# One more chunk of the MLP's second product as seven half-block products, and another order of all steps

## The chip, the cores and the metric

The kernel runs on one core of a Trainium2 chip. The metric is the device time of one execution in microseconds (us). The core has five queues of instructions: TensorE (PE, matrix products; its weight loads are shown apart as PEld), VectorE (DVE), ScalarE (ACT), GpSimd (POOL) and SyncE (SP), which issues nearly all transfers. Each queue works strictly in the order in which its instructions were written, and semaphores hold an instruction until what it reads is there and what it overwrites has been read.

## The reference

A recurrent attention (4 batches, 8 heads, 768 time steps, head size 40) is followed by a two-layer MLP with an exact GELU (320 to 2048 to 320) over 3072 tokens. The MLP's two weight matrices are of 64-bit floats; everything else is of 32 bits.

```python
for t in range(S):
    y[:, :, t] = np.einsum('bhd,bhde->bhe', rt, state)
    Sa = np.einsum('bhde,bhe->bhd', state, at)
    state_decay = state * wt[:, :, None, :] - np.einsum('bhd,bhe->bhde', Sa, bt)
    state = state_decay + np.einsum('bhd,bhe->bhde', vt, kt)
...
x = np.ascontiguousarray(attn_out.transpose(0, 2, 1, 3)).reshape(B * S, H * D)
...
h = x @ w_in
g = 0.5 * h * (1.0 + erf(h * inv_sqrt2))
return (g @ w_out).astype(np.float32)
```

## The kernel before

The sequence of 768 steps is cut into 12 chunks of 64. In each chunk the recurrence is turned into matrix products, for all 4 batches and 8 heads at once, and the chunk's 256 tokens (4 batches times 64 steps) then go through the MLP.

**Who sets the order.** The function `order` returns one long string of tokens such as `nm.3`, which means step `nm` of chunk 3. `perform` calls the steps in that order, and each writes its instructions to the queue it belongs to. The schedule is manual on all five queues, so the order of the tokens is the order on each queue. The argument `first_seven` (the constant `NS`) isn't used in `order`; what is done how is in the tokens themselves. PSUM is four banks, which `take` and `drop` hand out in the order of the tokens, so the order also decides which step waits for which bank.

**The steps of a chunk**, by their tokens:

- Loads on SP: `Lw La Lb Lk LV Lr` (w, a, b, k, v, r), from chunk 4 on others besides (`Lv Lwt Lbt Lkt`).
- Decays: `lg` (logarithm of w, ACT), `cu` and `wT` (running sums, PE), `ec` and `ew` (exponentials, ACT), `sa sb sk` (products with a, b, k; DVE or POOL). In the early chunks `ta tb tk tv tr` turn tiles over on PE, and `sn kc vc rc` copy them out of PSUM on ACT.
- Small products on PE, each followed by a masked copy on DVE: `nm`/`nk` (the matrix N that has to be inverted), `vm`/`vk`, `am`/`ak`.
- The inverse. For chunk 0 a loop of four squarings and a last product: `qm.0` to `qm.4` on PE, with `qc qz qb qa` on ACT and DVE between them, and `ql` (a transpose, L996) at the end. From chunk 1 on 32x32 blocks go through DRAM (`Ns`, `Nl`) to POOL, which solves them (`ic`, L907 and L909), and back (`Is`, `If`, `Ij`); `tc_` (L1007) turns them, and `jm jc km kt0 kt1` join blocks to 64x64.
- The chunk's result: `av xm` (PE), `xc0 xc1` (copies), `sm` (product with the inverse), `sc` (copies), `pk pb` (new state and output), `oa od om` (DVE), `tm tn oc` (the state turned over for the next chunk), `ym yc`. `om` writes the output, times a decay, into `xt`, the MLP's input, and `ox` completes `xt` with 11 small transfers.
- The MLP: `mh.c.p` for p from 0 to 7 is the first product (L1231, 20 records each in the trace, since each product of 32-bit floats appears as two), `ge` the GELU on ACT. The second product of the first three chunks is `pm.c.0` to `pm.c.3` (L1347: eight matmuls of 128x320 each), copied out by `pc`. From the fourth chunk on it is `m1` to `m7` (L1270): the 2x2 blocks of GELU output and weights go through Winograd's form of Strassen's scheme, seven products of half blocks (eight matmuls of 128x160 each) instead of eight. Its sums are `s1` to `s4` on DVE, `e1` to `e6` on ACT and DVE, and once, for the weights, `ws.0` to `ws.3`. `so` writes the output.

**The weights** come as 64-bit floats. There are 26 units (0 to 9 are the first matrix, 10 to 25 the second), loaded by `Lf`, `Lf5` and `Ls`, and converted with integer operations: `cp cm cs` on DVE and `ce` on ACT, and then in one of three ways: `cv` (two DVE instructions), or `cl cn` (ACT) with `cg` (two POOL instructions), or `cl cn` with `cx` (two products with the identity on PE) and `cy` (one on DVE). Before the change no unit goes the third way, though the steps are there.

**Products of constants.** `warm.4.i` is one matmul of the identity with four copies of a mask (128x512, two records), whose result nobody reads; `warm_first` is three such products.

The lines named here and below: L1231 `mh`, L1236 `ge`, L1270 `m1` to `m7`, L1347 `pm`, L1223 the sums of the seven products, L1220 `ws`, L845 the masked copies, L588 `cp`, L602 `cm`, L609 `cs`, L617 and L618 `cv`, L595 `ce`, L640 and L641 `cg`, L1007 `tc_`, L996 `ql`, L1164 `om`, L1176 and L1179 `ox`. L196 is the helper `mm`, which writes most small products.

```python
def perform(steps, token):
    name, *numbers = token.split(".")
    steps[name](*(int(n) if n.isdigit() else n for n in numbers))
...
    @step
    def warm(n, i):
        pt = take(f"warm{i}")
        mm(pt[:, 0, :n * P], ident, cum_m.unsqueeze(1).to_broadcast([P, n, P]))
        drop(f"warm{i}")
```

Of the kernel before, what the change touches and what calls it, by code (L numbers as in the profile page):

```python
# [16 lines left out]
def order(chunks, first_seven):  # L17
    return """
        of_half_set Lw.0 pads_a.0 sums_mask lg.0 cu.0 ec.0 Lb.0 sb.0 warm_set pads_w.0 pads_extra.2 pads_extra.0
        pads_extra.1 identity upper_mask pads_rows.0 pads_r.0 pads_VR.1 pads_r.1 first_ones.0 Tt_zero bias_set  # L20
        pads_a.1 pads_w.1 first_ones.1 pads_VR.0 wT.0 warm.4.18 ew.0 tb.0 sn.0 La.0 Lf.0.1.0 ta.0 sa.0 nm.0 nk.0
        qt Lw.1 Lf.3.1.0 lg.1 wT.1 ew.1 warm.4.26 qm.0 warm.4.16 cu.1 Lf.1.0.0 Lf.0.0.1 Lf.0.0.0 Lf.3.0.0 cl.3
        Lf.1.1.0 Lf5.1.0 Lb.1 La.1 Lf.2.1.0 Lf.0.1.1 Lf5.0.1 Lk.0 qi.0.p pads_extra.3 qi.1.v cp.1 cp.0 qc.0 ce.1
        qz.0 cm.1 qb.0.0.v qb.0.1.a qm.1 qc.1 cs.1 cv.1 cm.0 cm.3 cp.3 warm_first Lr.0 Lf.2.0.0 Lf5.0.0 LV.0
        Lf.2.0.1 Lf.2.1.1 Lf5.1.1 Lk.1 warm.4.11 qa.1 qz.1 qb.1.0.v ce.0 cn.3 ce.3 ec.1 qb.1.1.a cs.0 cs.3 sb.1
        qm.2 qa.2 qz.2 qb.2.0.v warm.4.3 ta.1 warm.4.19 tb.1 iz.1 cg.3 sk.0.p sa.1 cp.5 cv.0 cm.5 cl.5 qc.2
        qb.2.1.a qm.3 qz.3 qb.3.0.v qa.3 tk.0 ce.5 sn.1 nm.1 kc.0 qb.3.1.a cn.5 nk.1 cs.5 cp.2 tr.0 cg.5 qm.4
        rc.0 ce.2 cl.4 qc.3 cl.7 tv.0 qa.4 cs.2 cp.7 cm.2 ce.7 cm.7 cn.7 ql cs.7 am.0 jm.0 ak.0 cv.2 cp.4 cm.4
# [12 lines left out]
        ce.23 kc.2 cs.23 cv.23 cp.25 pm.0.0 mh.0.6 mh.0.7 cl.20 cn.20 ce.20 cs.20 cm.25 ce.25 cs.25 cv.25 tc_.1
        unused.a unused.v cg.20 ge.0.2 jm.1 vm.2 iz.2 ic.2.0.4 ic.2.4.8 ic.2.8.12 ic.2.12.16 ic.2.16.20
        pads_rows.1 ic.2.20.24 onward_set ic.2.24.28 ic.2.28.31 cp.22 ce.22 cs.22 cm.22 Ls.14 Lw.3 cv.22 cm.24
        jc.1 km.1 vk.2 ge.0.3 kt1.1 La.3 Lr.3 pm.0.1 kt0.1 sm.1 cp.24 unused.r sc.1.1 sc.1.0 lg.3 cu.3 ec.3 ce.24
        ta.3 cs.24 cv.24 am.2 pk.1 pb.1 Lk.3 Lv.3 Lb.3 pm.0.3 pm.0.2 La.4 oa.1.1 om.1.1 oa.1.0 om.1.0 od.1.0 sb.3
        od.1.1 sk.3.v pc.0.1 pc.0.0 ak.2 ox.1.0 ox.1.1 tb.3 tm.1 wT.3 oc.1 sn.3 tn.1 av.2 ym.2 ew.3 yc.2 mh.1.2
        sa.3 tv.3 nm.3 nk.3 xm.2 ta.4 mh.1.3 LV.3 so.0.0 Lwt.4 Ns.3.0 Is.2.0.s Is.2.1.s Ns.3.1 Lb.4 If.2.1 If.2.0
        Ij.2.1 Ij.2.0 so.0.1 Nl.3.1 Nl.3.0 tc_.2 tr.3 Lbt.4 Lr.4 ge.1.1 mh.1.6 mh.1.7 mh.1.0 xc1.2 xc0.2 ge.1.3
        mh.1.4 mh.1.1 ge.1.0 jm.2 tk.3 jc.2 km.2 kt1.2 kt0.2 kc.3 mh.1.5 ge.1.2 sm.2 sc.2.0 sc.2.1 tb.4 pk.2 am.3
        pb.2 tr.4 oa.2.1 pm.1.0 vm.3 oa.2.0 od.2.0 od.2.1 om.2.1 om.2.0 tw.4 ak.3 vk.3 Lb.5 Lw.4 Lkt.4 La.5  # L50
        ox.2.1 Lv.4 LV.4 tm.2 pm.1.1 oc.2 tn.2 lt.4 pw.4 ew.4 en.4 av.3 ym.3 yc.3 sn.4 sa.4 pm.1.3 xm.3 nm.4
        pc.1.1 pm.1.2 ox.2.0 tv.4 xc1.3 nk.4 vm.4 ta.5 pc.1.0 vk.4 tk.4 Ns.4.1 Ns.4.0 so.1.1 mh.2.6 mh.2.0 mh.2.7
        mh.2.2 mh.2.1 xc0.3 lg.4 ge.2.3 iz.3 ic.3.0.4 ic.3.4.8 ic.3.8.12 ic.3.12.16 ic.3.16.20 ic.3.20.24
        ic.3.24.28 ic.3.28.31 Is.3.1.p Is.3.0.p Nl.4.0 Nl.4.1 iz.4 ic.4.0.4 ic.4.4.8 ic.4.8.12 ic.4.12.16
        ic.4.16.20 ic.4.20.24 ic.4.24.28 ic.4.28.31 Is.4.1.p Is.4.0.p iz.5 If.3.1 If.3.0 Lwt.5 Ij.3.1 Ij.3.0 kc.4
        tc_.3 am.4 jm.3 mh.2.3 ge.2.0 jc.3 km.3 tw.5 ak.4 kt1.3 ge.2.1 kt0.3 lt.5 Lr.5 Lk.4 mh.2.4 sm.3 tr.5
        sc.3.1 sc.3.0 mh.2.5 pk.3 pb.3 cu.4 ge.2.2 pw.5 pm.2.0 pm.2.2 oa.3.1 om.3.1 od.3.1 oa.3.0 od.3.0 tm.3
        Lv.5 Lbt.5 Lkt.5 so.1.0 Lw.5 om.3.0 tb.5 oc.3 ec.4 ew.5 en.5 tn.3 av.4 ym.4 yc.4 ws.0 lg.5 sa.5 pc.2.0
        tv.5 sn.5 pm.2.1 nm.5 La.6 ox.3.1 Lk.5 ox.3.0 xm.4 pm.2.3 sk.4.p nk.5 Ns.5.0 Ns.5.1 If.4.0 If.4.1 Nl.5.1
        Nl.5.0 Lwt.6 Ij.4.0 Ij.4.1 xc0.4 tk.5 ws.1 kc.5 xc1.4 one_set vm.5 am.5 vk.5 tc_.4 pc.2.1 ak.5 ta.6  # L60
        mh.3.0 mh.3.1 jm.4 mh.3.6 jc.4 ge.3.0 km.4 kt0.4 mh.3.7 ge.3.3 Lbt.6 Lr.6 kt1.4 sm.4 sc.4.1 sc.4.0 sb.4
        cu.5 mh.3.2 pk.4 pb.4 LV.5 so.2.1 so.2.0 tr.6 tw.6 tb.6 ec.5 lt.6 Lkt.6 mh.3.3 mh.3.4 mh.3.5 ge.3.1
        ge.3.2 m1.3 m2.3 oa.4.0 oa.4.1 od.4.1 ws.3 od.4.0 tm.4 oc.4 tn.4 av.5 ym.5 om.4.0 pw.6 om.4.1 s1.3 s2.3
        s4.3 e1.3 ew.6 Lv.6 La.7 Lw.6 ox.4.1 ic.5.0.4 ic.5.4.8 ic.5.8.12 ic.5.12.16 ic.5.16.20 ic.5.20.24
# [1321 lines left out]
```

## Time and profile before

| what | value |
|---|---|
| median of 3 runs | 672.73 us (672.18 to 674.0) |
| the profiled execution | 673.18 us |
| its span on the core, first to last instruction | 671.5 us |
| mean granted clock of TensorE | 0.982 |
| PE busy | 643.9 us, 96% |
| DVE / ACT / POOL busy | 421.5 / 262.9 / 382.7 us |
| transfers | 78.10 MB, mean 116 GB/s |
| chain that ended last | PE 80%, of it L1231 28%, L196 22%, L1270 21%, L1347 8% |

The costliest groups of PE:

| line | what | records | busy, us |
|---|---|---|---|
| L1231 | first product of the MLP | 1920 | 222.9 |
| L1270 | seven products of nine chunks (four groups) | 1008 | 147.2 |
| L1347 | second product of three chunks | 192 | 54.3 |
| L196 | products of constants (128x512) | 18 | 12.3 |

How to read it: the span is what the profile covers, and the time of an execution is a little longer (673.18 against 671.5 us). A busy time is the union of an engine's instructions; since matmuls overlap, the mean duration of one times their number is more than the busy time. The page also has a picture of the span in 40 equal slices, in which a digit is the busy share in tenths; one slice is 16.8 us. In the answers of the trace "idle before <- X" is the time in which an engine stood before an instruction, and X what ended that time; "issue" means that the profile shows nothing it waited for.

### The profile page before, as it was taken

The page shows a single profiled execution, that of the slowest core. Times are in us where ns is not written, and L with a number is a line of the kernel's source. Part 1 is how long each engine was busy: PE and PEld are TensorE (multiplying, and loading weights), DVE is VectorE, ACT ScalarE, POOL GpSimd, SP SyncE. Part 2 cuts the span into 40 slices and gives each one's busy share as a digit, 9 for nine tenths or more (in the row PEclk, how much of TensorE's full clock was granted, in tenths as well). Part 3 has the DMA queues.
Part 4 walks back from the last instruction along what each step waited for, and adds up shares of the span by engine and source line. Part 5 has one row for each costly group of instructions (what it writes and reads, how often), then busy time and mean ns, then how long its engine had stood idle before and what let it go on. Part 6 is the DMA issues. An engine that isn't in the chain of part 4 may idle for free.

```text
span 671.5 us, 28177 instructions
## 1 busy us (share of the span) xinstructions
PE 643.9 (96%) x12480; PEld 560.8 (84%) x12480; DVE 421.5 (63%) x528; ACT 262.9 (39%) x329; POOL 382.7 (57%) x803
## 2 busy tenths in 40 slices
PE   4797889999999999999999999999999999999997
PEld 3576778888778878898898998997998988988987
DVE  1699988671664755885884777773885863723403
ACT  4456636522352452552623545242252344033040
POOL 4245873780585873871886860884872877830000
PEclk9796979999999999999999999999999999999999
DMA  9989488848867758647949757748658564130100
GB/s 153 159 169 163 98 189 170 152 91 137 151 112 138 137 109 148 138 86 136 155 85 163 141 115 136 124 86 155 130 108 141 109 121 84 38 60 3 26 16 21
DMA packets 302934, 78.10 MB, mean 116 GB/s; under 512 B 282556, under 2 KB 297692, under 8 KB 302812
## 3 DMA queue, kind: packets, MB, share of 16 engines
q1 hardware_dynamic: 301748, 73.78, 60.2%
q0 software_dynamic: 864, 2.36, 2.1%
q8 instruction: 98, 1.61, 1.0%
q14 instruction: 24, 0.20, 0.1%
q10 hardware_dynamic: 200, 0.16, 0.1%
HBM read 62.62 MB, written 9.70 MB: 108 GB/s over the span
## 4 chain that ended last, share of the span: by engine, by line
PE 80%; DVE 4%; SPq 2%; DMA 2%; issue 2%; POOL 1%; ACT 1%; DVEq 0%; POOLq 0%; ACTq 0%
PE bank L1231 28%; PE bank L196 22%; PE bank L1270 21%; PE bank L1347 8%; PE bank L731 2%; DMA v_pairs<-in_w_dram 1%; SPq L446 1%; POOL tmp L907 1%; DVE conv L609 1%; DMA T<-inv_blocks 1%; POOL W L909 1%; SPq L886 1%; DVE conv L588 0%; DVE kT L737 0%; DVE conv L602 0%
## 5 line engine op out<-in xcount | busy, mean ns | idle before, releaser
L1231 PE MATMUL bank<-xt,w_in_sb 64*128 64x256 f32 x1920 | 222.9, 384 | 0.1
L1231 PEld LDWEIGHTS bank<-xt,w_in_sb 64*128 64x128 f32 x1920 | 182.9, 188 | 25.2 <-issue 2.1
L907 POOL TENSOR_TENSOR tmp<-W,Nb 128x126 f32<-128x126 f32 (+22 forms) x341 | 151.7, 445 | 91.0 <-DMA Nb<-N_blocks 65.2
L909 POOL TENSOR_TENSOR W<-W,tmp 128x126 f32<-128x126 f32 (+22 forms) x341 | 160.4, 470 | 26.7
L1236 ACT ACTIVATE gt<-bank 128x1024 f32<-128x1024 f32 x48 | 48.9, 1023 | 104.5 <-PE bank L1231 104.4
L1270 PE MATMUL bank<-w_out_sb,gt 128*128 128x160 f32 x576 | 83.7, 301 | 0.0
L1270 PEld LDWEIGHTS bank<-w_out_sb,gt 128*128 128x128 f32 x576 | 79.2, 190 | 3.0 <-issue 2.0
L1347 PE MATMUL bank<-w_out_sb,gt 128*128 128x320 f32 x192 | 54.3, 437 | 0.7 <-issue 0.7
L1347 PEld LDWEIGHTS bank<-w_out_sb,gt 128*128 128x128 f32 x192 | 35.7, 190 | 15.6 <-issue 1.4
L1108 DVE TENSOR_TENSOR SM<-bank,upper 128x832 f32<-128x832 f32 x24 | 23.7, 1019 | 19.4 <-PE bank L196 19.3
L1007 DVE STREAM_TRANSPOSE conv<-Tt 128x512 f32<-128x512 f32 x11 | 7.8, 709 | 36.5 <-DMA Tt<-inv_blocks 36.4
L1056 DVE COPY Tt<-bank 32x512 f32<-32x512 f32 x9 | 6.2, 689 | 34.4 <-ACT Tt L1056 32.9
L898 POOL MEMSET W<- 128x512 f32 x11 | 5.8, 530 | 38.2 <-DMA inv_blocks<-W 38.2
L701 DVE TENSOR_TENSOR_SCAN kT<-spare,kT 128x256 f32<-128x256 f32 x32 | 24.1, 813 | 3.5 <-ACT kT L694 3.5
L1270 PE MATMUL bank<-extra,conv 128*128 128x160 f32 x176 | 25.7, 300 | 0.0
L1223 DVE TENSOR_TENSOR os<-os,bank 128x160 f32<-128x160 f32 x36 | 11.4, 318 | 22.6 <-PE bank L1270 12.1
L1158 DVE TENSOR_TENSOR st<-bank,st 128x832 f32<-128x832 f32 (+1 forms) x22 | 21.0, 981 | 6.4 <-PE bank L196 6.4
L1270 PEld LDWEIGHTS bank<-extra,conv 128*128 128x128 f32 x176 | 24.4, 190 | 0.2
L1223 DVE TENSOR_TENSOR conv<-gt 128x1024 f32<-128x1024 f32 x9 | 11.7, 1297 | 20.3 <-ACT gt L1236 20.3
L595 ACT ACTIVATE conv<-conv,rebias 128x320 uint32<-128x320 uint32 (+1 forms) x26 | 16.0, 622 | 21.2 <-DVE conv L588 21.2
L196 PEld LDWEIGHTS bank<-SM,Tt 64*64 64x64 f32 x768 | 17.5, 133 | 6.2 <-issue 3.4
L1236 ACT ACT_TABLE_LOAD x17 | 21.8, 1283 | 1.1 <-DVE N L845 0.8
(212 smaller groups left out, 1120.4 us busy)
## 6 DMA issues: line engine op xcount, KB each, us to landing
Nb<-N_blocks SPq DMA_DIRECT2D x22, 256.0 KB
b_rows<-in_b_dram SPq DMA_DIRECT2D x24, 160.0 KB
k_rows<-in_k_dram SPq DMA_DIRECT2D x24, 160.0 KB
VR<-in_v_dram SPq DMA_DIRECT2D x24, 160.0 KB
out_dram<-os SPq DMA_DIRECT2D x48, 80.0 KB
Tt<-inv_blocks SPq DMA_DIRECT2D x44, 64.0 KB
a_pairs<-in_a_dram SPq DMA_DIRECT2D x18, 144.0 KB
r_pairs<-in_r_dram SPq DMA_DIRECT2D x36, 72.0 KB
```

The lines of the kernel that those rows point to most:

```text
L196: nc.tensor.matmul(o, lhsT, rhs, start=first, stop=True, skip_group_check=True)
L595: nc.scalar.activation(power, power, ACT.Relu, bias=rebias, scale=8.0)
L701: nc.vector.tensor_tensor_scan(logs[:, at:at + n], onward, logs[:, at:at + n], 0.0, ALU.mult, ALU.add)
L907: nc.gpsimd.tensor_tensor(t, W[:, :rows, j:j + 1].to_broadcast([P, rows, rest]), Nb[:, j:j + 1, j + 1:].to_broadcast([P, rows, rest]), ALU ...
L909: nc.gpsimd.tensor_tensor(W[:, :rows, j + 1:], W[:, :rows, j + 1:], t, ALU.add)
L1108: nc.vector.tensor_tensor(SM[:, g], pair_of(f"S{c}_", g).rearrange("p x i c -> p i x c"), pass_upper.unsqueeze(1).unsqueeze(1).to_broadcas ...
L1158: nc.vector.tensor_tensor(to, pair_of(f"QY{c}_", g)[:, :, :, cols], to, ALU.add)
L1223: nc.vector.tensor_tensor(to, one_, other, how)
L1231: nc.tensor.matmul(ph[:, x, s], w_in_sb[half(x), kt, p * P:(p + 1) * P], xt[half(x), kt], start=kt == 0, stop=kt == NK - 1)
L1236: nc.scalar.activation(gt[:, 4 * q:4 * q + 4].rearrange("p (x s) t -> p x s t", x=2), bank(f"ph{c}_{q}").rearrange("p x (s t) -> p x s t", ...
L1270: nc.tensor.matmul(po[:, n, :DM // 2], l_[:, f], r_[:, f], start=f == 0, stop=f == NF // 2 - 1)
L1347: nc.tensor.matmul(po[:, g, :DM], gt[:, f, g * P:(g + 1) * P], w_out_sb[:, f], start=f == 0, stop=f == NF - 1)
```

## The change

Nothing is changed but the string of tokens and the constant `NS`. The string holds 1515 tokens before and 1535 after. As sets they differ in this:

```
removed   pm.2.0 pm.2.1 pm.2.2 pm.2.3  pc.2.0 pc.2.1
added     m1.2 to m7.2  s1.2 to s4.2  e1.2 to e6.2
removed   warm: three of 9        added   warm: twelve, 18 in all
units 0, 11      cv            becomes  cl cn cx cy
unit 8           cv            becomes  cl cn cg
units 5, 9, 16, 21   cl cn cg  become   cv
```

All the other tokens are the same, in another order. The diff, cut to its core:

```diff
-        of_half_set Lw.0 pads_a.0 sums_mask lg.0 cu.0 ec.0 Lb.0 sb.0 warm_set pads_w.0 pads_extra.2 pads_extra.0
...
+        identity sums_mask warm.4.7 Lf.0.1.0 Lf.0.0.0 cm.0 cp.0 warm.4.5 cn.0 cl.0 warm.4.9 warm.4.1 warm.4.28
+        of_half_set pads_VR.1 warm.4.27 warm_set pads_VR.0 onward_set cx.0 warm_first Lw.0 first_ones.0 bias_set
...
-    NS = 3
+    NS = 2
```

The order on PE, up to the first products of the second chunk's join, as it follows from the two strings:

```
before  cu.0 wT.0 warm.18 tb.0 ta.0 nm.0 wT.1 warm.26 qm.0 warm.16 cu.1 qm.1 warm_first warm.11 qm.2 warm.3 ta.1
        warm.19 tb.1 qm.3 tk.0 nm.1 tr.0 qm.4 tv.0 am.0 jm.0 warm.10 vm.0 km.0 av.0 sm.0 pk.0 pb.0
        wT.2 tk.1 tm.0 warm.29 cu.2 tr.1 tv.1 ta.2 warm.12 am.1 vm.1 mh.0.2 mh.0.3 av.1 ym.1 mh.0.0 tb.2 xm.1
        nm.2 mh.0.1 tv.2 mh.0.4 mh.0.5 tr.2 tk.2 pm.0.0 mh.0.6 mh.0.7 jm.1
after   warm.7 warm.5 warm.9 warm.1 warm.28 warm.27 cx.0 warm_first cu.0 wT.0 ta.0 tb.0 nm.0 warm.20 warm.26 tk.0
        qm.0 warm.11 warm.0 warm.25 qm.1 cu.1 wT.1 am.0 qm.2 warm.3 tv.0 qm.3 warm.21 ta.1 tb.1 qm.4 tr.0 nm.1
        vm.0 jm.0 tr.1 av.0 km.0 warm.29 tv.1 sm.0 tk.1 vm.1 warm.10 pk.0 pb.0
        am.1 cu.2 wT.2 warm.16 cx.11 tm.0 av.1 ym.1 warm.23 tb.2 ta.2 tr.2 xm.1 nm.2 mh.0.2 mh.0.3 mh.0.0 mh.0.6
        mh.0.7 mh.0.1 mh.0.4 mh.0.5 tv.2 pm.0.0 pm.0.1 jm.1
```

On DVE, from the inverse loop to the first chunk's output `om.0`:

```
before  qz.0 cm.1 qb.0 cs.1 cv.1 cm.0 cm.3 cp.3 qa.1 qz.1 qb.1 cs.0 cs.3 sb.1 qa.2 qz.2 qb.2 sa.1 cp.5 cv.0 cm.5
        qz.3 qb.3 qa.3 nk.1 cs.5 cp.2 qa.4 cs.2 cp.7 cm.2 cm.7 ql cs.7 ak.0 cv.2 cp.4 cm.4 cp.9 vk.0 cs.4 cm.9
        kt1.0 sk.1 cs.9 xc1.0 cm.6 cp.6 cs.6 sc.0.1 sc.0.0 cv.6 od.0 od.0 om.0.1 cp.8 om.0.0
after   qz.0 cm.1 qb.0 cs.1 cv.1 qz.1 cs.2 qa.1 cm.2 qb.1 cm.3 cp.3 cv.2 cs.3 qa.2 qz.2 qb.2 sb.1 cp.4 cm.4 cp.5
        qa.3 qz.3 cm.5 cs.4 qb.3 sa.1 cs.5 cv.5 qa.4 ql cp.6 nk.1 cm.7 vk.0 ak.0 cm.6 cs.6 cp.7 cv.6 cs.7 cm.8
        cp.8 xc1.0 kt1.0 sk.1 cm.9 cs.8 cp.9 sc.0.1 sc.0.0 cs.9 cv.9 vk.1 cp.11 cp.10 od.0 om.0.0 om.0.1
```

On SP, up to the transfers that complete the first chunk's `xt`:

```
before  Lw.0 Lb.0 La.0 Lf.0.1.0 Lw.1 Lf.3.1.0 Lf.1.0.0 Lf.0.0.1 Lf.0.0.0 Lf.3.0.0 Lf.1.1.0 Lf5.1.0 Lb.1 La.1
        Lf.2.1.0 Lf.0.1.1 Lf5.0.1 Lk.0 Lr.0 Lf.2.0.0 Lf5.0.0 LV.0 Lf.2.0.1 Lf.2.1.1 Lf5.1.1 Lk.1 Ls.2 Ns.1.1
        Lf.1.0.1 Lf.1.1.1 Ns.1.0 Lw.2 Lf.3.1.1 Nl.1.0 Nl.1.1 Ls.0 Lf.3.0.1 Lr.1 LV.1 Ls.1 Ls.3 La.2 ox.0.1 ox.0.0
after   Lf.0.1.0 Lf.0.0.0 Lw.0 La.0 Lb.0 Lk.0 Lf.1.1.0 Lf.2.1.0 Lf.2.0.0 Lf.1.0.0 Lw.1 Lf5.0.0 Lf.3.1.0 Lf.0.1.1
        Lf.3.0.0 LV.0 Lf5.0.1 Lf.0.0.1 Lf.3.0.1 Lb.1 La.1 Lf.1.1.1 Lf5.1.0 Lr.0 Lf.2.0.1 Lf.2.1.1 Lf.1.0.1 Lf.3.1.1
        Lr.1 LV.1 Lf5.1.1 Lk.1 Ns.1.1 Ns.1.0 Ls.0 Ls.1 Lw.2 Nl.1.0 Nl.1.1 Lr.2 Ls.3 Ls.4 Ls.2 Lb.2 La.2 ox.0.1 Ls.5
        ox.0.0
```

On PE around chunk 2's second product:

```
before  pk.3 pb.3 cu.4 pm.2.0 pm.2.2 tm.3 av.4 ym.4 pm.2.1 nm.5 xm.4 pm.2.3 vm.5 am.5 mh.3.0
after   pk.3 pb.3 mh.2.4 mh.2.5 m1.2 m2.2 tm.3 m5.2 av.4 ym.4 m6.2 xm.4 nm.5 mh.3.0 mh.3.1 m3.2 m7.2 m4.2 vm.5 am.5
```

## The prediction

> **What bounds the kernel now.** I read first the page's sums and slices, then stretches of 4 us over the start, then TensorE's (PE's) instructions in order of time, then the chain of waits.
>
> ```profile
> span 671.5 us, 28177 instructions
> ...
> PE 643.9 (96%) x12480; PEld 560.8 (84%) x12480; DVE 421.5 (63%) x528; ACT 262.9 (39%) x329; POOL 382.7 (57%) x803
> ...
> PE   4797889999999999999999999999999999999997
> ...
> DVE  1699988671664755885884777773885863723403
> ...
> DMA  9989488848867758647949757748658564130100
> GB/s 153 159 169 163 98 189 170 152 91 137 151 112 138 137 109 148 138 86 136 155 85 163 141 115 136 124 86 155 130 108 141 109 121 84 38 60 3 26 16 21
> ```
>
> A slice is 16.8 us. PE idles 27.6 us (671.5 - 643.9). In the stretches of 10 us 20.6 of them lie before 100 us, 4.2 behind the last product, and only 2.8 between. So from 105 us on the time is the sum of PE's work, and all else is the start. There the DMA engines are nearly full for 67 us (mean 161 GB/s) and VectorE (DVE) is 84 to 99% busy from 40 to 100 us.
>
> ```profile
> 20.00:24.00 4.00, 0.32 (x6) 0.14 (x5) 3.92 (x5) 0.78 (x2) 3.77 (x6) 0.92 1.12 124
> 24.00:28.00 4.00, 3.62 (x125) 2.62 (x126) 1.08 (x4) 1.50 (x3) 0.09 (x1) 0.50 0.88 174
> ...
> 60.00:64.00 4.00, 4.00 (x103) 3.61 (x98) 3.94 (x6) 1.49 (x3) 2.56 (x3) 0.50 1.18 167
> ...
> 92.00:96.00 4.00, 4.00 (x98) 3.71 (x92) 3.97 (x8) 1.67 (x3) 3.45 (x8) 0.50 0.89 192
> ```
>
> Columns: stretch, length, busy PE, PE's weight loads, DVE, ACT, POOL, granted clock, DMA share, GB/s. Three times PE ran on half a clock.
>
> ```profile
> 24.38 1.92 PE L196 MATMUL bank<-N,st 32*32 32x32 f32 x123 [3.43 <-issue]
> ...
> 84.28 4.59 PE L1231 MATMUL bank<-xt,w_in_sb 64*128 64x256 f32 x40
> 90.80 2.30 PE L196 MATMUL bank<-VR,late 64*64 64x104 f32 x64 [1.92 <-DVE late L845]
> ...
> 122.19 0.75 PE L196 MATMUL bank<-conv,spare 32*32 32x32 f32 x64
> ```
>
> The landmarks: qm.0 at 24.38, the first MLP product mh.0.2 at 84.28, av.1 waiting on ak.1, and jm.1 at 122.19. Before jm.1 the start decides, behind it PE's work.
>
> ```profile
> 232.03 8.81 PE bank L1347 x32
> ...
> 244.24 4.50 PE bank L1347 x16
> ...
> 251.26 4.50 PE bank L1347 x16
> ...
> 282.57 4.54 PE bank L1270 x32
> ...
> 290.51 4.54 PE bank L1270 x32
> ...
> 296.64 6.72 PE bank L1270 x48
> ```
>
> These are chunk 2's four half products (17.81 us) and chunk 3's seven (15.80 us).
>
> **The seven products.** Removed 17.81, added 15.80 of PE: -2.0 us. Beside them come s1 to s4 (four of 1.22 to 1.39 us by the DVE groups L1223) and seven small additions (0.32 to 0.36), less two copies of 0.48: +6.7 us of DVE, and three small ACT copies (0.29). DVE is busy 16.5 of 25 us at 225 to 250, so 8 us per stretch cover them. m5.2 stands 10 us of PE work behind pb.3 (two mh of 2.36, m1, m2, a turn), while DVE has ws.0, oa, od, om and s1.2 to do, some 8 us. Cover gone, it is up to +4.7 net. I take -2.0. Sums of weights (ws) only move.
>
> **What PE still has to do at jm.1.** From the two orders, after jm.1 starts the new one has left the seven products (15.80), tk.2 (1.04) and one product of constants (1.02); the old has pm.2 (17.81) and pm.0.1 (4.45), which the new one does earlier. That is 4.4 us less. So the new kernel breaks even if jm.1 starts at 122.2 + 4.4 = 126.6, and each us earlier is a us won, if later waits are alike.
>
> **Up to the inverse loop.** Two w_in loads go ahead of Lw.0: 0.91 + 0.65 us of issue, and 0.52 MB at 198 GB/s (10 to 20 us), so the logarithm lg.0, which PE waits for until 7.66, comes up to 2.7 us later. Six products of constants and cx.0 now stand ahead of cu.0, in time in which PE waits anyway; cu.0 and wT.0 took 2.47 + 1.99 us at the start and 1.24 + 1.11 at 72 to 77 us, so 2.1 us come back; warm.18 (1.69) no longer stands before tb.0. nm.0: 16.9 + 2.7 - 2.1 - 1.7 = 15.8. nk.0 and qt take 3.7 more, so qm.0 could start at 19.5. The idle 3.43 us marked "issue" belong to no step; they may return or not: 19.5 to 23, I take 20.5, as only one such gap in the start is that long.
>
> **The loop (qm.0 to ql).** Now 28.2 us (24.4 to 52.6). I added DVE's instructions inside it by their rows (0.41 for cp or cm, 0.69 cs, 1.37 cv, 0.71 qz, 0.7 qb, 0.69 qa, 1.22 a mask): 22.7 before, 22.0 after. But nk.1 and a longer run of conversions no longer sit ahead of a qa or ql; what is in front of each step of the loop fits beside qm's 2.08 us. 25 to 28, I take 26.5: ql ends at 47, 5.6 us earlier.
>
> **ql to the end of pb.0.** Now 19.7 us. New on DVE: eight cp/cm (3.3), three masks (3.7), three cs (2.1), a cv (1.4), xc1 and kt1 (1.7), sk.1 (1.4), sc (2.0), 15.4, then pb.0 1.7: 17.1; POOL at work beside it stretches such instructions (a cp of 320 columns takes 0.49 us at 77 to 99 us and 0.32 at 105 to 118), and u6's and r's loads must be there: 17 to 22, I take 19. pb.0 ends at 66 (before 72.3).
>
> **pb.0 to jm.1.** Added by rows, PE has 18.4 us up to the end of nm.2 and 29.8 us from mh.0.2 to jm.1 (eight mh 18.9, tv.2 2.0, two pm 8.9). In the old order four turns and products (tk.1, tr.1, tv.1, vm.1: 5.2 us) and pm.0.1's place differ: this is where PE work is moved into idle time. mh.0.2 waits for xt: om.0 ends 5.7 us of DVE behind sc, 7.2 stretched, so 71.5; the 11 ox transfers took 8.2 us to issue, Ls.5 between them 1.6, landing 1: 82. But all loads before them on SP's queue are 12.9 MB (before 11.9), 80 us at 161 GB/s, so 82 to 86. nm.2 ends at 66 + 18.4 + 1 = 85.4. I take 87 for mh.0.2, and 1 us of waits behind it: jm.1 at 117.8. Behind jm.1, waits of the new order's own: 1 us (the old has 2.8 between 105 and the tail).
>
> What is queued behind mh.0.2 if it is late: all PE, and ge.0.1, behind which xc1.1 frees the bank for mh.0.4. The weights of pm.0 need units 10 to 17; DVE has about 10 us of work to cv.16 behind sa.2, against 21 of PE: covered. jm.1 also needs the last unit (tc_.1 is behind cv.25, 33 us of DVE behind om.0, 40 stretched: 111) and POOL's ic.1, which took 32.6 us and may start at 63: covered by 6.
>
> **Sum.** 126.6 - 117.8 - 1.0 = 7.8 us (of these 2.0 are the products). Span 671.5 - 7.8 = 663.7; the profiled execution took 673.18, 1.7 more than its span: 665.4. The runs' median, 672.73, lies 0.45 lower: **665.0**. Seven weight units change their way of conversion (0, 5, 8, 9, 11, 16, 21: three fewer on POOL, more on DVE and PE); they are in the lists above. one_log, with a table load of 1.28 us on ACT, moves to chunk 6: ACT is busy 9.6 of 25 us at 425 to 450, so it costs nothing, and 1.3 if that cover were gone.
>
> The nine further products of constants and cx cost 12 us of PE in idle time; uncovered, in the stretch pb.0 to jm.1, they cost 1 each, and are in the 18.4.
>
> **Rivals.**
> (1) *PE stands on half a clock between ql and pb.0.* PE has about 15 us of work at full clock in those 19, with gaps; 56 to 64 us were at 0.50 before. At half, some 6 us of it double, pb.0 ends 3 later: 668. Against: two products of constants stand there. The Trainium skill, page "TensorE: Matmul & The Clock Gate", Part 1, states that an idle window of some 3.4 us drops the clock to half and as long a busy one restores it; this trace agrees (3.43 us idle, then 0.50 at 24 to 28), and by that rule gaps of under 3 us, as I count them, leave the clock up.
> (2) *The start does not move.* Loads or the loop keep pb.0's end at 72.3: mh.0.2 at 72.3 + 19.4 = 91.7, jm.1 at 122.5, won 4.1 - 1.0: 669.6. For: DMA at 0.9 and more.
> (3) *The new DVE work of chunk 2 falls on PE's path*: +6.7 against the 7.8: 671.7. Against: DVE's free time there.
> (4) *xt is late, slower than before.* ox.0 is last of 12.9 MB on one queue, which also stops at Ns.1 until nk.1 is done, and at Nl.1. It decides from mh.0.2 at 94.8 on (126.6 - 1.0 - 30.8), a mean rate under 136 GB/s. The fifth slice had 98, if for want of requests. xt at 101 gives jm.1 131.8: 672.7 + 5.2 + 1 = 679. Against: 161 over four slices.
>
> **Numbers.** 665 has 0.56 (own range 660 to 669), rival 1 0.11, 2 0.11, 3 0.08, 4 0.14. With 0.3% (2 us, about what runs of this kernel tell from no change), faster takes the first three less some spill, 0.76; same 0.09; slower 0.15. Range 658 (xt at 84, no issue gap, loop 25: 6 more) to 676 (rival 4 half way).
>
> **What would show it.** Right: PE's first instruction of L1231 near 87 with all eight mh (x160) close behind, jm.1 near 118, ql (L996) near 47, chunk 2's second product as 112 records of L1270 instead of 64 of L1347. Wrong: idle PE in front of the first L1231 put down to DMA xt; clock 0.5 at 50 to 66; more than 5 us of PE idle between 120 us and the tail; the first L1231 after 95.

## The result, and the profile after

The changed kernel takes 679.54 us (median of four, 677.68 to 680.26), the one before beside it 673.37 us (672.18 to 674.20): a ratio of 1.0089, interval 1.0061 to 1.0117. The forecast was 665.0, so the change made the kernel 6 us slower instead of 8 us faster. All line numbers of the new kernel are higher by one (L1232 is `mh`, L1271 the seven products, L1348 `pm`, L1008 `tc_`, L197 the helper `mm`).

The page's sums and slices of the profile after, whose execution took 677.68 us:

```profile
span 676.0 us, 28315 instructions
...
PE 651.5 (96%) x12554; PEld 569.3 (84%) x12554; DVE 429.0 (63%) x541; ACT 266.1 (39%) x332; POOL 375.4 (56%) x797
...
PE   8897999999999989999999999999999999999997
...
PEclk9999999799999989999999999999999999999999
```

PE's first slices rose from 4797 to 8897, as the change set out to do, and its idle time fell from 27.6 to 24.5 us. But busy PE rose by 7.6, where the seven products should have lowered it by 2. The products of constants (12.3 us before, 20.1 now) and the new `cx` (3.5 us in four rows) outweigh what the second product saves: idle time of the start is now filled, mostly with work that nobody reads. PE's instructions in order of time (start, length, then the group, its records and the wait ahead of it):

```profile
19.80 1.16 PE L197 MATMUL bank<-aT,nT 40*64 40x64 f32 x64 [1.85 <-DVE aT L754]
...
23.68 1.55 PE L197 MATMUL bank<-N,st 32*32 32x32 f32 x128
...
87.97 17.94 PE L1232 MATMUL bank<-xt,w_in_sb 64*128 64x256 f32 x160
105.84 1.97 PE L197 MATMUL bank<-ident,VR 128*64 128x128 f32 x32
107.74 8.88 PE L1348 MATMUL bank<-w_out_sb,gt 128*128 128x320 f32 x32
118.69 1.02 PE L197 MATMUL bank<-conv,spare 32*32 32x32 f32 x64 [2.07 <-DVE conv L1008]
...
247.49 6.27 PE L1232 MATMUL bank<-xt,w_in_sb 64*128 64x256 f32 x40 [1.91 <-DMA xt<-xt]
```

These are nm.0, qm.0, mh.0.2 with all eight `mh` behind it, tv.2, two `pm`, jm.1 and, far behind, mh.3.0. The first MLP product and jm.1 stand within 1 us of the forecast (87 and 117.8). By its own sum the kernel should now be 7.9 us ahead (126.6 - 118.7); it ends 4.5 us behind (span 676.0 against 671.5). So 12.4 us went behind jm.1. Where, is read from both kernels' windows, cut at the starts of jm.1, jm.3, jm.4, jm.6 and jm.11 (columns: stretch, length, PE busy and its records, granted clock, DMA share, GB/s). Before:

```profile
0.00:122.19 122.19, 101.61 (x2013) 0.90 0.87 159
122.19:218.34 96.15, 94.59 (x2011) 1.00 0.70 127
218.34:262.24 43.90, 43.90 (x890) 1.00 0.71 129
262.24:366.80 104.56, 104.46 (x2003) 1.00 0.71 129
366.80:605.87 239.07, 237.89 (x4814) 1.00 0.60 110
```

After:

```profile
0.00:118.69 118.69, 106.00 (x2044) 1.00 0.90 166
118.69:212.95 94.26, 93.33 (x1983) 0.96 0.69 123
212.95:262.44 49.49, 46.51 (x955) 0.97 0.70 122
262.44:367.44 105.00, 103.80 (x2050) 1.00 0.70 128
367.44:612.55 245.11, 242.64 (x4788) 1.00 0.58 107
```

From jm.1 to jm.11 PE idles 2.84 us before (length less busy, lines two to five) and 7.58 after: 4.7 us of new waits. The clock, full throughout before, is lost twice behind such a wait. Windows of 4 us of the new kernel, with the same columns:

```profile
116.00:120.00 4.00, 1.93 (x79) 0.85 0.86 129
120.00:124.00 4.00, 4.00 (x131) 0.50 0.57 107
124.00:128.00 4.00, 4.00 (x72) 0.79 0.50 100
...
248.00:252.00 4.00, 4.00 (x24) 0.57 0.87 149
```

If time at a lower clock is work not done, these windows lose 4 x 0.15 + 4 x 0.50 + 4 x 0.21 + 4 x 0.43 = 5.2 us. That would leave some 2.5 us in no named wait. The experiments below show that the 5.2 are too many.

In this profile both waits come from the new order's own queues. At jm.1 DVE stood idle for the transfer of the inverse, and the reason is the queue of SP. DVE, then SP's issues (SPq), each in order of time:

```profile
117.83 0.71 DVE L1008 STREAM_TRANSPOSE conv<-Tt 128x512 f32<-128x512 f32 x1 [2.56 <-DMA Tt<-inv_blocks]
```

```profile
102.97 2.01 SPq L887 DMA_DIRECT2D N_blocks<-N  x4
105.08 0.99 SPq L566 DMA_DIRECT2D k_rows<-in_moe_w_out_dram  x2
106.12 1.99 SPq L566 DMA_DIRECT2D w_out_sb<-in_moe_w_out_dram  x2
108.21 1.29 SPq L915 DMA_DIRECT2D inv_blocks<-W  x2
```

POOL had ended ic.1 at 100.0; `Is.1`, which takes its result to DRAM, is issued at 108.21 behind Ns.2 and two weight loads. At mh.3.0 it is DVE and SP: the forecast counted on 8 us of free DVE in 25, but the windows from 225 to 250 us show, before and after (busy PE, PEld, DVE, ACT, POOL, then the clock):

```profile
225.00:250.00 25.00, 25.00 (x472) 19.50 (x468) 16.50 (x19) 12.14 (x13) 18.94 (x40) 1.00 0.69 132
```

```profile
225.00:250.00 25.00, 23.09 (x432) 21.48 (x426) 24.66 (x25) 9.27 (x13) 20.05 (x30) 0.97 0.67 120
```

DVE is busy for 24.66 of the 25. The weights' sum ws.0 (1.65 us) stands ahead of om.3, which then ends at 233.4, and on SP La.6 (3.02 us of issue) ahead of ox.3.0.

### The profile page after: what moved, and what is told of

It reads as the page before. It is cut to its first block, busy times and chain, and to the rows that moved or that the text cites. A ratio compares the mean times of both kernels' runs of the same rounds, so it can differ in the third digit from the quotient of the medians.

```text
span 676.0 us, 28315 instructions
## 1 busy us (share of the span) xinstructions
PE 651.5 (96%) x12554; PEld 569.3 (84%) x12554; DVE 429.0 (63%) x541; ACT 266.1 (39%) x332; POOL 375.4 (56%) x797
## 3 DMA queue, kind: packets, MB, share of 16 engines
q0 software_dynamic: 864, 2.36, 2.0%
## 5 line engine op out<-in xcount | busy, mean ns | idle before, releaser
L1232 PE MATMUL bank<-xt,w_in_sb 64*128 64x256 f32 x1920 | 223.5, 384 | 2.2 <-DMA xt<-xt 1.9
L1232 PEld LDWEIGHTS bank<-xt,w_in_sb 64*128 64x128 f32 x1920 | 185.3, 188 | 24.6 <-DVE spare L846 2.0
L910 POOL TENSOR_TENSOR W<-W,tmp 128x126 f32<-128x126 f32 (+22 forms) x341 | 159.6, 468 | 26.7
L1271 PE MATMUL bank<-w_out_sb,gt 128*128 128x160 f32 x640 | 92.0, 301 | 0.0
L1271 PEld LDWEIGHTS bank<-w_out_sb,gt 128*128 128x128 f32 x640 | 87.8, 190 | 3.7 <-issue 2.8
L1348 PE MATMUL bank<-w_out_sb,gt 128*128 128x320 f32 x128 | 35.9, 436 | 0.0
L1348 PEld LDWEIGHTS bank<-w_out_sb,gt 128*128 128x128 f32 x128 | 23.8, 190 | 9.6 <-issue 0.2
L1008 DVE STREAM_TRANSPOSE conv<-Tt 128x512 f32<-128x512 f32 x11 | 7.7, 701 | 35.6 <-DMA Tt<-inv_blocks 35.5
L1271 PE MATMUL bank<-extra,conv 128*128 128x160 f32 x192 | 27.9, 300 | 0.0
L1271 PEld LDWEIGHTS bank<-extra,conv 128*128 128x128 f32 x192 | 26.5, 190 | 0.2
L770 POOL TENSOR_TENSOR k_rows<-k_rows,part 128x640 f32<-128x640 f32 x8 | 12.5, 1568 | 24.5 <-DMA k_rows<-in_k_dram 24.1
L197 PEld LDWEIGHTS bank<-SM,Tt 64*64 64x64 f32 x768 | 18.5, 135 | 7.4 <-issue 6.1
L197 PE MATMUL bank<-SM,Tt 64*64 64x104 f32 x768 | 21.7, 255 | 2.5 <-DVE SM L1090 1.6
L1306 ACT COPY os<-bank 128x160 f32<-128x160 f32 x10 | 2.9, 293 | 53.6 <-PE bank L1271 42.7
```

Source lines behind the costliest of these rows:

```text
L197: nc.tensor.matmul(o, lhsT, rhs, start=first, stop=True, skip_group_check=True)
L770: (nc.vector if q == "v" else nc.gpsimd).tensor_tensor(to, rows(k_of(c)), decays(c), ALU.mult)
L910: nc.gpsimd.tensor_tensor(W[:, :rows, j + 1:], W[:, :rows, j + 1:], t, ALU.add)
L1008: nc.vector.transpose(L_tile, flat(Tt)[:, :, :BL])
L1232: nc.tensor.matmul(ph[:, x, s], w_in_sb[half(x), kt, p * P:(p + 1) * P], xt[half(x), kt], start=kt == 0, stop=kt == NK - 1)
L1271: nc.tensor.matmul(po[:, n, :DM // 2], l_[:, f], r_[:, f], start=f == 0, stop=f == NF // 2 - 1)
```

## The experiments

The edits are shown as moves of tokens in the string; all have the change's code. Ratios are to the kernel before on the same chip, whose runs scatter by some 0.4% there, so intervals are wide. "Lead" in the expectations is the difference of the two profiles at a product, plus the difference in the work that PE then has left (4.4 us at jm.1). e1 and e4 are read by their ratios alone. The experiments' kernels have lower line numbers (`mm` is L190 to L192, the seven products L1264 to L1266).

**Both kernels again.** The unchanged kernels, run with the later experiments.

> The kernel before, unchanged, profiled a second time. Theory A (the profile that the prediction read was typical): jm.1 starts at 121 to 123 us again and PE's clock falls to 0.50 at 92 to 96. Theory B (its start was slower by chance, since the same order reached jm.1 at 116.5 in h2_old_start): jm.1 at 115 to 120 and no half clock at 92 to 96; the time within 1 us of the other runs of the kernel before.

> The changed kernel, unchanged, profiled a second time on the chip of old_again. Both theories: 0.6 to 1.1% over the kernel before. Theory A: jm.1 3 to 5 us ahead of old_again's. Theory B: jm.1 within 3 us of it, and the same waits as in the first profile (at jm.1 on DVE conv, at mh.3.0 on xt, at km.3 and km.9 on T, at jm.5 on late).

Measured: old 1.0001 (0.9978 to 1.0024), span 673.4; new 1.0056 (1.0023 to 1.0090), span 677.1. The loss is there again, somewhat smaller. The old kernel's profile reaches jm.1 at 120.4 this time, the new one's at 120.1. For old_again the landmark lies just above theory B's 115 to 120, and the half clock at 92 to 96 came again, as in A; for new_again B holds, as the two starts are 0.3 us apart. Of the first profile's waits, those at jm.1 (2.90 us), at jm.5 (2.36) and on T (4.3 in all) are there again. The one at mh.3.0 is not:

```profile
247.50 2.72 PE L1232 MATMUL bank<-xt,w_in_sb 64*128 64x256 f32 x20
```

The stretch from jm.1 to the last product's end is as long all the same (552.8 us, 553.1 in the first profile).

**The first wait: Is.1 ahead of the load.**

```diff
-Ls.15 ... Is.1.1.s Is.1.0.s ... Ls.14 ... Ij.1.1
+Is.1.1.s Is.1.0.s Ls.15 ... Ij.1.1 Ls.14
```

> The changed kernel with one edit on SP's queue: Is.1 goes ahead of Ls.15 and Ls.13, and Ls.14 behind If.1 and Ij.1, so that the inverse of chunk 1 comes back sooner. Theory A (the wait of 2.07 us before jm.1 also let PE's clock fall to half for some 6.8 us, and both are lost time): If.1 issues 1 to 3 us sooner, tc_.1 by 116, the clock stays at 1.00 from 116 to 128, and the time falls by 2.1 + 3.0, to 674.5. Theory B (only the idle time counts, the half clock falls where PE has nothing urgent): 677.5. Theory C (the loss lies elsewhere): 679.5.

Measured: 1.0020 (0.9987 to 1.0053). Better than the new order's 1.0056 to 1.0089, within the intervals, and not faster than before. It is nearest to theory A (674.5, a ratio of 1.0017; B's 677.5 is 1.0061).

**The clock held up.** Two products of constants ahead of jm.1 and two ahead of mh.3.0.

```diff
+warm.4.40 warm.4.41 jm.1
+warm.4.42 warm.4.43 mh.3.0
```

> The changed kernel with four products of constants more on PE: two in front of jm.1 and two in front of mh.3.0, the two places where PE idled 2.07 and 1.91 us and its granted clock then was 0.50. The waits themselves stay. Theory A (the idle stretch is what halves the clock): granted clock 1.00 from 116 to 128 and from 248 to 252, and 3.0 + 1.7 us won: 674.8. Theory B (the half clock has another cause, or costs nothing): within 1 us of 679.5. Theory C (the added products delay what they stand before): 681 or more.

Measured: 1.0082 (1.0047 to 1.0116), span 676.5. The clock stayed full at both places; the windows of this kernel:

```profile
116.00:120.00 4.00, 4.00 (x82) 1.00 0.81 130
120.00:124.00 4.00, 3.98 (x163) 1.00 0.59 109
124.00:128.00 4.00, 3.78 (x122) 1.00 0.51 96
```

No time was won, as theory B had it. The pair at jm.1 takes 1.88 us, about the wait that it fills, so only the pair at mh.3.0 (1.12 us each) is new work behind jm.1. From jm.1 to the last product's end this profile takes 553.1 us, as the first one of the new order did. So the full clock gave back some 2 us there, not 4.7 or 5.2.

**The two orders joined at jm.1 and at jm.5.** h1 is the new order up to jm.1 and the old rest; h2 the reverse. x4 is the new order up to jm.5 and the old rest, x5 the reverse. (x2 and x3, first forms of x4 and x5, compute the third chunk's second product in both ways, so their times, 1.0298 and 1.0418, say nothing of the orders.)

> The new order up to and with jm.1, then all steps that are left in the old order (chunk 2's second product as four half products again). Theory A (the new start is worth 7 to 8 us and the loss is in the new order behind jm.1): 673.4 - 6.9 for the start, + 3 for the half clock behind the wait at jm.1 = 669.5. Theory B (a start that ends sooner only meets the same waits later, whatever the order): 676 to 679.

> The old order up to and with jm.1, then all steps that are left in the new order (chunk 2's second product as seven products). Theory A (the new order behind jm.1 loses 9 us against its own sum of work, some 12.3 less the half clock at jm.1): 673.4 + 9 - 2 (the seven products and what else the sets differ in) = 680 to 682. Theory B (the new order behind jm.1 is no worse than the old, and what is lost comes of starting it sooner): 671 to 674.

> The new order up to the first product of the sixth chunk's inverse (jm.5), with the third chunk's seven products in it, the old order of the rest behind it. If the loss lies ahead of jm.5 (chunk 2's seven products, xt at mh.3.0, the half clock at jm.1): 1.004 to 1.009, as the new order. If the later part loses as much: 1.000 to 1.003.

> The old order up to jm.5 with four products of the third chunk, the new order of the rest behind it. If the loss lies ahead of jm.5: 0.997 to 1.002. If the later part loses 4 to 5 us, as the profiles' leads say (0.4 us ahead at jm.5, 4.3 behind at jm.11): 1.005 to 1.008.

Measured: h1 1.0094 (1.0065 to 1.0124), h2 1.0082 (1.0047 to 1.0117), x4 1.0107 (1.0064 to 1.0150), x5 1.0131 (1.0095 to 1.0168). All four are as slow as the new order or slower, where one half at fault would have left one of each two near 1.000. So they don't say which half is at fault: a joint has waits of its own. PE in h1 and in x4, just behind the joint:

```profile
120.99 1.06 PE L726 MATMUL bank<-ident,extra 128*128 128x128 f32 x8 [2.26 <-DVE extra L764]
```

```profile
317.77 0.26 PE L191 MATMUL bank<-T,Js 32*32 32x32 f32 x2 [3.56 <-DMA T<-inv_blocks]
```

In h1 tk.2 waits for the load Lk.2, which the new order issues later than the old rest wants it. What the runs do give is how the same start varies. The old start stood at jm.1 at 122.2 (before), 120.4, 117.1 (e5), 116.5 (h2), 119.2 (x3), 118.4 (x5) and 115.9 (x7); the new one, where unchanged, at 118.7 (after), 120.1, 118.9 (e3), 118.0 (h1), 120.8 (x2), 119.0 (x4) and 120.3 (x6). The means are 118.5 and 119.4. The profile on which the forecast was built is the latest of the seven.

**The seven products by themselves.** e3 is the new order with chunk 2's second product in four parts, the sums ws put where the old order has them; e5 the old order with the seven products in chunk 2.

```diff
-m1.2 m2.2 ... m5.2 ... m6.2 ... m3.2 m7.2 m4.2   (with s1-s4, e1-e6)
+pm.2.0 pm.2.2 ... pc.2.0 ... pm.2.1 ... pm.2.3 ... pc.2.1
```

> The changed kernel with chunk 2's second product as four half products again, at the places of m1, m2, m6 and (ahead of mh.3.0) m3, and the weights' sums ws spread over chunks 2 and 3 as in the old order. Theory A (the seven products cost more in waits than they save: DVE's sums delay om.3, ox.3 and mh.3.0): the wait for xt at mh.3.0 and the half clock behind it go, 3.6 us, against 2.0 us more of PE's work: 1.6 us less than the changed kernel. Theory B (they save what PE's rows say): 2.0 us more than the changed kernel.

> The kernel before with the seven products in chunk 2 alone, its order otherwise kept; the sums of the weights move ahead into chunk 2. Theory B (prediction: -2.0 us of PE's work, covered on DVE): 2 us less than the kernel before. Theory A (DVE is not free between pb.3 and nm.5: 6.7 us of sums and 4.6 us of weights' sums come into a stretch of 18 us of PE's work): PE waits in front of m5.2 or nm.5, and the time is 2 to 6 us over the kernel before.

Measured: e3 1.0156 (1.0115 to 1.0197), e5 1.0127 (1.0086 to 1.0167). Four products are slower than seven in the new order, by 1.0% of new_again, and seven slower than four in the old order, by 1.3%. Both lie above both of their expectations. Four products in the new order's places don't mend it, so nothing here says that the seven are what makes it slow. It looks as if each order were fitted to its own form, and a product put in by hand cost more by its place than by its work; these two runs suggest that and don't show it. In e5 one such place is seen: chunk 4's ym.4 waits 4.18 us for a copy on ACT.

```profile
239.99 1.99 PE L190 MATMUL bank<-rT,turned 40*64 40x64 f32 x64 [4.18 <-ACT turned L1196]
```

**The waits mended.** e4 has ws.0 and La.6 moved back; x1 all of the new order's waits that the profile named.

```diff
 e4:  -ws.0 ... om.3.1          +om.3.1 ws.0
      -La.6 ... ox.3.0          +ox.3.0 La.6
 x1 besides, with the moves of e1:
      -Lwt.5 Ij.3.0 Ij.3.1      +Ij.3.0 Ij.3.1 Lwt.5
      -tc_.6 ak.7               +ak.7 tc_.6
      -Nl.10.0 Nl.10.1 Ij.9.1   +Ij.9.1 Nl.10.0 Nl.10.1
```

> The new order with two moves ahead of the fourth chunk's first MLP products: on VectorE the first sum of the third chunk's MLP (ws.0) behind the second masked copy om.3.1, on SyncE the load La.6 behind the write ox.3.0. Theory 'own waits' (the loss of the new order behind the second chunk's inverse comes from waits that its own queue order makes, each one local): the wait of 1.91 us for xt at mh.3.0 and the clock of 0.57 behind it go, jm.4 starts 3 to 4 us sooner than in the new order's profile (262.4), and the ratio to before is 1.005 or less, 3 us below the new order. Theory 'slack elsewhere' (what is won at one place is waited for at the next, since loads and the inverse's trips through memory have their own pace): the wait goes, jm.4 comes sooner, but jm.6 (367.4) is where it was within 1 us and the ratio stays at 1.006 to 1.010.

> The new order with all of its own waits behind the second chunk's inverse mended: the issues of Is.1 ahead of the load Ls.15 and Ls.14 behind Ij.1, ws.0 and La.6 as in e4_xt3, the load Lwt.5 behind the two Ij.3, the masked copy ak.7 ahead of the transposition tc_.6, Ij.9.1 ahead of the loads Nl.10. Theory 'own waits': these waits add up to some 2.1 + 1.9 + 1.0 + 1.2 + 1.0 us and the half clock behind the first two to 4.6 us, so the kernel ends 8 to 11 us below the new order, at 0.992 to 0.998 of before, and beats both. Theory 'slack elsewhere': no more than 3 us below the new order, ratio 1.002 to 1.009.

Measured: e4 1.0038 (0.9999 to 1.0078), x1 1.0023 (0.9989 to 1.0058), span 673.6. x1 is the best form of the new order, some 2 to 4 us below it, and level with the kernel before. Its page has a full clock throughout (0.999), and the two named waits are gone: Is.1 is issued at 104.36, and jm.1 and mh.3.0 start with no wait.

```profile
span 673.6 us, 28317 instructions
...
PE 648.4 (96%) x12554; PEld 564.2 (84%) x12554; DVE 427.3 (63%) x541; ACT 266.5 (40%) x332; POOL 379.9 (56%) x797
...
PEclk9999999999999999999999999999999999999999
```

Yet PE still idles 9.4 us between jm.1 and jm.11. What PE waits for most between 117 and 611 us (total, times, longest):

```profile
PE bank L191 <- DMA T<-inv_blocks: 3.3, 3, 1.4
PE bank L191 <- issue: 1.4, 2, 0.8
```

The waits are now many and small, the largest still for the inverse blocks from DRAM (in old_again's answer for this stretch that one is 0.6). e4's ratio is what "own waits" expected, but its interval also holds the other theory's range. x1's is what "slack elsewhere" expected: by "own waits" it should have beaten both kernels. Mending pays, but only about a third of what the waits' sum promised. And it hardly shortens the stretch that it was meant for. From jm.1 to the last product's end, in before, after, e2_fill and x1_mend (columns as above):

```profile
122.19:667.27 545.08, 542.25 (x10470) 1.00 0.58 107
118.69:671.80 553.11, 545.53 (x10510) 0.99 0.58 105
119.18:672.31 553.13, 544.26 (x10515) 1.00 0.59 105
117.20:669.43 552.23, 542.83 (x10511) 1.00 0.58 106
```

With a full clock and without the two named waits x1_mend is 0.9 us shorter there than after, and it idles 9.4 us instead of 7.6. As far as one profile of each can say, the mended waits are waited off elsewhere, and what the clock gave back doesn't show. The other 1.5 us by which its span is shorter come from an earlier jm.1 (117.2).

**Is PE the bound behind jm.1?** If the other engines set the pace there, a lead is worth nothing and more PE work is free.

```diff
-mh.1.3
+mh.1.3 warm.4.40 warm.4.41 warm.4.42 warm.4.43 warm.4.44 warm.4.45
```

> The new order with six more products of constants on TensorE (two of them took 1.88 us in an earlier profile, so about 5.6 us) between jm.1 and jm.2, behind the second chunk's MLP product mh.1.3. Theory 'PE is the bound behind jm.1': they cost their time, 5.6 us, so the ratio is 1.014 to 1.018. Theory 'the other queues set the pace' (TensorE's lead of 5 to 8 us at jm.1 is waited off anyway): they cost 2 us or less, ratio 1.006 to 1.011, and the idle time of PE between jm.1 and jm.11 falls from about 8 us to about 3.

> The old order with the same six products of constants behind mh.1.3. PE idles only 2.9 to 5.0 us between jm.1 and jm.11 in the two profiles of the old order. Theory 'PE is the bound behind jm.1': +5.6 us, ratio 1.008 to 1.009. Theory 'the other queues set the pace': +2 us or less, ratio 1.000 to 1.003; between the two it is a mixture, by the idle time that goes.

Measured: new 1.0121 (1.0083 to 1.0159), old 1.0073 (1.0044 to 1.0102). The six products took 5.42 us in both profiles. In the old order they cost 4.9 us, nearly their time; in the new order 2 to 4 us over its 1.0056 to 1.0089, between the two expectations. So PE is the bound behind jm.1 in the old order. In the new one the ratio leaves it open, and the idle time speaks for the bound. The windows of x6 between jm.1 and jm.11:

```profile
120.29:218.13 97.84, 97.84 (x1994) 0.97 0.69 122
218.13:263.41 45.28, 44.44 (x954) 1.00 0.67 122
263.41:373.63 110.22, 107.34 (x2051) 0.97 0.71 126
373.63:621.71 248.08, 243.10 (x4790) 1.00 0.59 105
```

Idle is 0 + 0.8 + 2.9 + 5.0 = 8.7 us, not the 3 that "the other queues set the pace" wanted. So the new order waits as much without its lead as with it, which makes them waits of the order itself.

**A better joint, and fewer constants.** x8 is h1 with Is.1 and Lk.2 issued sooner and tk.2 later; x9 is x1 without six of the 18 products of constants.

```diff
 x8, with the moves of e1:
      -Ij.1.0 Ij.1.1 Lk.2 jm.1 sk.2.v tk.2 kc.2
      +Lk.2 If.1.0 ... jm.1 ... vk.2 sk.2.v ... ce.24 tk.2 kc.2
 x9:  -warm.4.11 warm.4.0 warm.4.3 warm.4.29 warm.4.23 warm.4.4
```

> The new order up to jm.1, with the issues of Is.1 ahead of the load Ls.15 and the load Lk.2 ahead of If.1, then the old order's rest (four products in the third chunk), with sk.2, tk.2 and kc.2 put behind vk.2 and the conversion ce.24, where the new order has them. If the new start is worth its lead (5.4 to 7.9 us over the old profile at jm.1) and the old rest keeps it: 663 to 668 us, ratio 0.988 to 0.994. If the lead at jm.1 is mostly a late draw of the one old profile (other runs of the old start reached jm.1 at 115.9 to 120.4, against 122.2): 0.996 to 1.001. If the seam still waits as in h1: 1.004 or more.

> x1_mend without six of the 18 products of constants (two of the three behind qm.0 at 25.2, those at 37.4, 57.7, 82.4 and 123.8 us; 6.4 us of PE by their rows). If they lie on TensorE's path they give it back: 3 to 6 us below x1_mend (1.0023), 0.993 to 0.998. If they only fill waits, nothing changes, 1.000 to 1.004, or it becomes slower where the clock falls behind the waits.

Measured: x8 1.0035 (0.9997 to 1.0072): the joint costs less than in h1, but still waits (6.4 us of idle PE between jm.1 and jm.3), and the clean question, the new start with an undisturbed old rest, stays open. x9 1.0089 (1.0056 to 1.0121), slower than x1 by some 4 us (the two were measured against separate runs of the kernel before). With less work on PE its profile is later already at jm.1 (120.3 against 117.2), and the page shows lost clock in the start:

```profile
PEclk9898999799997999999999999999999999999999
```

One profile of each could be chance. But over all runs the mean granted clock is 0.985 in x9 and 0.993 in x1, a difference of 5 us in 680, about what x9 lost.

## Why the prediction was wrong

**The step that failed is "1 us of waits behind jm.1"**, together with the premise of its landmark, "if later waits are alike". From jm.1 to the last product's end the old order took 545.1 us (before), 548.9 (old_again) and 550.1 (x7, its 5.42 us of constants taken off), the new one 553.1 (after), 552.8 (new_again) and 555.2 (x6, likewise). The means are 548.0 and 553.7, and the new order has 4.4 us less to do there: it loses 10 us where 1 was forecast. What the 10 are made of is known in part. Idle PE from jm.1 to jm.11 is 7.6, 8.6 and 8.7 us in the new order (after, new_again, x6) against 2.8, 5.1 and 5.6 in the old, so 4 of them are waits, though not the same ones each time. The clock takes up to 5.2 us in the windows of after; but e2 (551.0 us without the pair at mh.3.0) and x1 (552.2) keep it full and lose 7 to 9 us nonetheless, so it is worth some 2. The other 3 to 4 are PE busy for longer at a full clock than the rows of the forecast add up to (542.8 us in x1, where the old order's mean of 543.5 less 4.4 is 539.1). These parts are rough, since the old order alone spreads by 5 us. The profile of before could not show these waits, since they come from neighbours on queues whose new order was only followed up to jm.1. The two largest of after could have been found by the same means as the start: what stands on SP ahead of Is.1, and on DVE and SP ahead of om.3 and ox.3. Finding them would not have saved the change, as x1 shows.

**The landmark itself rested on one draw.** 126.6 was 122.2 + 4.4, with 122.2 from one execution; the mean of seven old starts is 118.5. Break-even was thus 122.9, and the new start's mean of 119.4 is worth 3.5 us, not 8. What the new order was to win back is partly what that execution happened to lose: up to jm.1 its mean clock was 0.90, in x7, with the same start, 0.96. Over the whole execution the clock is on the new order's side: its runs beside old_again have a mean granted clock of 0.991, the kernel before 0.986.

Together: 3.5 won ahead of jm.1, 10 lost behind it, some 6.5 to the bad. The two comparisons of the kernels say 6 and 4.

**Step by step.** *Seven products, -2.0*: right in sign on PE. The groups of L1271 are up by 8.3 + 2.2 + 2.2 + 2.5 = 15.2 us of busy time, L1348 down by 18.4, so -3.2. But the cover of 8 us on DVE was not there (24.66 of 25 busy), as rival 3 had it; its price came as xt late at mh.3.0 and the clock behind it, 1.91 + 1.7, not as 6.7. *nm.0 at 15.8, qm.0 at 20.5*: 19.80 and 23.68, 3 to 4 us late; the six constants took 7.40 us, from 2.16 to 9.4 (six took 5.42 in x6), and cx.0 and `warm_first` behind them lasted to 13.9, so cu.0 came later than thought, 2.2 us behind its input (L666 on ACT, done at 11.53). The gap of 3.43 us did not return. *Loop 26.5*: from 23.68 to ql's end at 50.35, 26.7. *ql to pb.0 19*: ended near 72, against 66, nearly 22 us from ql, the upper bound (the forecast's list of DVE's work adds up to 15.6 as printed, not 15.4). *mh.0.2 at 87, jm.1 at 117.8*: 87.97 and 118.69, and the first is luck. pb.0 ended 6 us late, but from there PE had no wait for xt and needed 16.0 us, where 21 had been left. *The nine constants are in idle time*: mostly so, but for the 2.2 us at cu.0, and in x9 PE was slower without six of them. *Rival 1* (half clock between ql and pb.0) did not happen in this profile (it did in x9's, 0.50 at 64 to 68), nor did *rival 4* (xt of chunk 0 late): all eight products of `mh` ran in one piece. The forecast's own tests named the failure rightly: "more than 5 us of PE idle between 120 us and the tail".

What stays open: why PE is busy for 3 to 4 us longer, and why a mended order's waits come back as small ones (x1). One trace of the first is that records of the same form overlap less. The group of `sm`'s products in old_again and in x1_mend:

```profile
L196 PE MATMUL bank<-SM,Tt 64*64 64x104 f32 x768 | 20.1, 253 | 1.9 <-DVE SM L1089 1.3 <-ACT SM L1089 0.6
```

```profile
L191 PE MATMUL bank<-SM,Tt 64*64 64x104 f32 x768 | 21.9, 253 | 3.5 <-issue 1.4 <-DVE SM L1084 1.3 <-DVE Tt L1051 0.6
```

The 768 records are as long (253 ns) but cover 1.8 us more. Who holds them apart wasn't tried.

## What to carry to other kernels

When all steps are reordered, a sum over the start is half a forecast: follow each queue of the rest too, and ask at every product on the bound engine what is issued just ahead of its last input. Here waits of 1 to 3 us at several stages added some 4 us of idle time. But mend one and measure before you believe the sum: the named waits of this order were worth a third of what they added up to. A landmark from one profiled execution needs its spread; here the same start moved by 6 us from one execution to another, as much as the whole effect. Work moved into idle time of the start is not won if the steady part gets slower with the new order; whether it is won with an undisturbed rest, no run here shows (h1 and x8 have waits of their own).

## What the hardware showed unexpectedly

Short waits can halve TensorE's clock, and a wait of the same length can leave it full. In the profile after, the granted clock was 0.50 and 0.57 for the next 4 us behind idle times of 2.07 and 1.91 us. In e3_four the wait at jm.1 is as long, and the clock stays full; in h2_old_start 1.42 us of waiting is enough. First e3, then h2, each with the window behind the wait:

```profile
118.90 0.74 PE L191 MATMUL bank<-conv,spare 32*32 32x32 f32 x64 [2.05 <-DVE conv L1002]
...
120.00:124.00 4.00, 3.35 (x139) 1.00 0.66 120
```

```profile
124.95 2.50 PE L190 MATMUL bank<-w_tile,cum_m 128*128 128x320 f32 x4 [1.42 <-ACT gt L1230]
...
124.00:128.00 4.00, 3.05 (x20) 0.62 0.51 91
```

So between 1.4 and 2.1 us the length of one wait doesn't decide it in these runs, and what a short wait costs in clock differs from one execution to the next. The Trainium skill, page "TensorE: Matmul & The Clock Gate", Part 1, puts the drop behind an idle window of some 3.4 us. These traces have it behind shorter ones, as had the prediction's own lines (1.92 us idle at 90.80, then 0.50 at 92 to 96). So rival 1 was too kind when it took gaps of under 3 us to leave the clock up.

Products whose result nobody reads may be worth more than they cost: x9, with 6.4 us of them taken out, was slower than x1_mend by about 4 us, at a mean clock of 0.985 against 0.993. It depends on the place: in e2 four more of them kept the clock up and won nothing.
